# Rows sorted by expert for the second network; zeroing from 112 partitions, output scatters unordered, row numbers copied by VectorE

## The chip, the cores and the metric

The kernel runs on one core of a Trainium2 chip, in a single launch. The core has five engines, each with its own instruction stream: TensorE (PE: matmuls, and PEld for loading their weights), VectorE (DVE), ScalarE (ACT), GpSimd (POOL) and SyncE (SP, which here issues most DMAs). Engines wait for one another through semaphores; 16 DMA engines move data between DRAM and the on-chip memory (SBUF). Matmul results land in PSUM banks, from which VectorE or ScalarE take them. The metric is device time in microseconds (us) of one execution; lower is better.

## The reference, cut to what matters

```python
attn_out = _attn_ref(r, k, v, w, a, b)          # a recurrence over 768 steps, 4 x 8 heads of 40
x = attn_out.transpose(0, 2, 1, 3).reshape(3072, 320)

# first network: each token goes to one of 8 experts (320 -> 1024 -> 320)
logits = x @ w_gate
expert_idx = argmax(logits, 1)
probs = softmax(logits);  gate_w = probs[i, expert_idx[i]]
# token i is the pos[i]-th of its expert; dropped when pos[i] >= capacity (768)
h = maximum(disp[e] @ w1[e], 0);  y = h @ w2[e]
x[i] = gate_w[i] * y[expert_idx[i], pos[i]]     # 0 when dropped

# second network: one network for all tokens (320 -> 2048 -> 320)
h = x @ w_in
g = where(h > 0, h, exp(minimum(h, 0)) - 1)
out = g @ w_out                                 # float32, in the order of the tokens
```

## The kernel before

The program has three stretches. **Attention** (to about 445 us) works through 24 units of 128 tokens in an order written out by hand (`ORDER`, `slot(k)`): for each unit `x_out` gives 320 features and 8 router logits per token, `route` and `route_mm` find the token's expert and its row, and `scatter` writes the unit's 128 rows into the DRAM buffer `disp` with an indirect DMA on GpSimd (one row number per partition, from `SLOT`). `disp` has a region of rows for each expert. `zero_d` clears the first 448 rows (`SL`) of each region beforehand, and `zero` clears, in six pieces between units 8 and 13, the rows of the buffer `yd` that lie behind the first 8 x 448.

**The first network** (455 to 695 us) has one block of 448 rows per expert, in four groups of 112. Block.`load` fetches the rows from `disp`; `turn` and `prep` transpose them on TensorE (12 transposes, four after each of three steps, `pt`) and split them into a high and a low part, `XH`, `XL`, and `XS` for the last 64 features (float32 accuracy out of reduced-precision matmuls). A block has 8 steps f of 128 hidden units: `s1(f)` is 8 matmuls of 448 columns into a bank `ph`; `relu` makes the parts `H` (ScalarE) and `L` (VectorE); `s2`, two steps later, takes for each of the four row groups three matmuls of 320 columns (weights: 112 columns of `H` or `L`; moving: the second weight matrix) into the four banks `po`. After the last step the four banks are copied to `Y`, and one DMA writes them to `yd`, at 448 rows per expert. The weights come from DRAM in halves of an expert (`Weights.fetch`), and `split` makes their high part (ScalarE, L777) and low part (GpSimd, L780), a quarter per step, two halves ahead. In the same steps VectorE converts the second network's weights from 64-bit to 32-bit floats (`Convert.pieces`, L853 to L865), and `gates()` computes in small pieces each token's gate and the row of `yd` (`ROW`) that holds its result.

**The second network** (from 704 us) has six blocks of 512 tokens with 16 steps each, in the order of the tokens. `load` gathers the 4 x 128 rows by `ROW` out of `yd` (four indirect DMAs on GpSimd, L1158), VectorE multiplies them by the gate (L1163), and `turn` and `prep` transpose and split as before. `elu` is the activation; its last subtraction `L` is on GpSimd (L1008) except in the first five steps. `s2` runs three steps behind. The outputs leave from SP, two groups at a time (L1169). Both networks are driven by `run(blocks, ...)`, each by a call of its own: the second call begins with `bl[0].start()`, which loads, transposes and splits the first block with nothing beside it.

Engines work in program order. `experts` calls `extra(b, f)` at the end of each step, so the place of an instruction in its engine's queue is set by block and step. `overflow()` repeats the work for experts with more than 448 rows; with these data its loop does not run.

Of the kernel before, what the change touches and what calls it, by code (L numbers as in the profile page):

```python
# [20 lines left out]
D = 320  # L21
NTOK = 3072
SL = 448
ES = 8 * SL
NU = 24
# [92 lines left out]
def attention(tc, nc, e_in, v_tok, d_in, wg, disp, cst, ring, early, early_w, cv, cap):  # L118
# [12 lines left out]
    sh = [ring.tile(i, F32) for i in range(4)]  # L131
# [10 lines left out]
    zr = sh[0][:, 2578:2738]  # L142
# [412 lines left out]
    def x_out(u):  # L555
# [6 lines left out]
        XO = wk.tile([128, 4, 80], F32, tag="XO", name="XO", bufs=4)  # L562
        st["XO", u] = XO
        nc.scalar.copy(XO, pv[:, :, 0:80])
        yield
        nc.vector.tensor_reduce(cst["lg"][:, u], pv[:, :, 80:88].rearrange("p j e -> p e j"), axis=AX.X, op=ALU.add)
# [5 lines left out]
    def route(u, n=2):  # L572

        c, r = u // 2, slice(u % 2, u % 2 + n)
        LG, MX = cst["lg"][:, u:u + n], cst["mx"][:, u:u + n]
# [29 lines left out]
    def scatter(u):  # L605
        x = nc.gpsimd.indirect_dma_start(
            out=disp, out_offset=bass.IndirectOffsetOnAxis(ap=cst["slot"][:, u:u + 1], axis=0),
            in_=st.pop(("XO", u)).rearrange("p j e -> p (j e)"), in_offset=None).ins
# [5 lines left out]
    def zero(dst):  # L614
        nc.sync.dma_start(out=dst.rearrange("(p i) d -> p (i d)", p=128).rearrange("p (x d) -> p x d", d=160),
                          in_=zr.unsqueeze(1).to_broadcast([128, 8, 160]))

    def zero_d(e):
        nc.sync.dma_start(out=disp[e * ES:e * ES + SL, :].rearrange("(p i) d -> p (i d)", p=112).rearrange("p (x d) -> p x d", d=160),
                          in_=zr[0:112].unsqueeze(1).to_broadcast([112, 8, 160]))  # L620
# [6 lines left out]
    def warm(n):  # L627
        w = early_w.H[0]
# [37 lines left out]
    for k in range(KR, NU + 1):  # L666
# [17 lines left out]
def consts(p):  # L684
# [8 lines left out]
    c["lg"] = p.tile([128, 24, 8], F32, name="LG")  # L693
    c["mx"] = p.tile([128, 24], F32, name="MX")
    c["oh"] = p.tile([128, 2, 8, 12], BF, name="OH")
    c["slot"] = p.tile([128, 24], I32, name="SLOT")
    c["gate"] = p.tile([128, 24], F32, name="GATE")
    c["row"] = p.tile([128, 24], I32, name="ROW")
    c["pos"] = p.tile([128, 24], F32, name="POS")
    c["epos"] = p.tile([128, 24], F32, name="EPOS")  # L700
    c["tok"] = p.tile([128, 24], F32, name="TOK")
# [14 lines left out]
def set_rest(nc, c):  # L716
# [5 lines left out]
    for e in range(8):  # L722
        g.memset(c["desc"][:, e:e + 1], float(8 - e))
        g.memset(c["ebase"][:, e:e + 1], float(ES * e))
# [603 lines left out]
```

## Time and profile before

| | us |
|---|---|
| median of 3 runs (lowest to highest) | 1073.83 (1069.45 to 1074.62) |
| profiled execution, device time | 1081.15 |
| its span, first to last instruction | 1078.9 |
| TensorE busy in the span | 981.8 (91%) |
| VectorE, ScalarE, GpSimd busy | 711.3, 497.6, 635.5 |
| chain of waits: TensorE's share, at the lines of `s1` (L964) and `s2` (L979 to L981) | 44%; 21%, 8%, 7%, 7% |

The profile is one execution; its own time lies 7.3 us above the median. A matmul's shown duration includes its way through the array, so successive matmuls overlap: their pace is read from their start times, not from their durations. "Idle before, <- X" names what ended an engine's wait.

### The profile page before, as it was taken

Reading aid. Unit: us, or ns where it says so; the run is one execution under the profiler, and the core shown is the slowest. Engines: PE = TensorE matmul, PEld = TensorE weight load, DVE = VectorE, ACT = ScalarE, POOL = GpSimd, SP = SyncE. Lnnn points to the kernel's source line nnn. Section 1 sums busy time; section 2 is a strip of 40 time slices with the busy share of each in tenths; the row PEclk is TensorE's granted clock in tenths of the full one; section 3 lists DMA queues with packets and bytes.
Section 4 is the critical chain, followed back from the end, with each engine's and each line's share of the span. In section 5 each row is a group of like instructions: output and inputs, shape, how many; then the busy total and the mean of one; then the engine's idle time right before and its main releaser. Section 6 shows DMA issues by size and latency. Waiting matters only on the chain.

```text
span 1078.9 us, 25743 instructions
## 1 busy us (share of the span) xinstructions
PE 981.8 (91%) x10319; PEld 897.1 (83%) x10319; DVE 711.3 (66%) x1232; ACT 497.6 (46%) x968; POOL 635.5 (59%) x932
## 2 busy tenths in 40 slices
PE   5868888799799899888999999789999999999995
PEld 5758887798788789678999999768899899989985
DVE  8856657687664666538899972157675757666563
ACT  4646544566454334242343434345555554555452
POOL 4757839798986713474777776763444435353332
PEclk9858988899899989999999999979999999999998
DMA  6769675588674855575888774410100101010101
GB/s 165 157 171 206 156 145 92 145 143 201 148 176 94 200 137 114 160 188 150 239 237 227 197 203 144 140 43 7 38 13 7 44 1 49 1 50 1 26 1 28
DMA packets 187160, 125.21 MB, mean 116 GB/s; under 512 B 102776, under 2 KB 174968, under 8 KB 185400
## 3 DMA queue, kind: packets, MB, share of 16 engines
q1 hardware_dynamic: 182964, 106.53, 40.6%
q0 software_dynamic: 3168, 11.03, 3.2%
q10 hardware_dynamic: 900, 5.93, 2.2%
q8 instruction: 83, 1.36, 0.6%
q14 instruction: 45, 0.37, 0.1%
HBM read 86.73 MB, written 36.72 MB: 114 GB/s over the span
## 4 chain that ended last, share of the span: by engine, by line
PE 44%; DVE 4%; issue 3%; DMA 3%; POOL 2%; ACT 1%; SPq 1%; POOLq 0%; ACTq 0%; DVEq 0%
PE ph L964 21%; PE po L981 8%; PE po L980 7%; PE po L979 7%; POOL L L1008 1%; PE pt L937 1%; DMA ring<-in_w_dram 1%; DMA S<-in_w_in_dram 1%; DVE L L994 1%; SPq L796 1%; DVE E L854 1%; DVE N L853 1%; POOL ring L780 0%; DVE N L864 0%; DVE M L862 0%
## 5 line engine op out<-in xcount | busy, mean ns | idle before, releaser
L780 POOL TENSOR_TENSOR ring<-ring,ring 128x176 fp32r<-128x176 f32 x320 | 200.1, 660 | 76.5 <-ACT ring L777 76.5
L1008 POOL TENSOR_TENSOR L<-E,H 128x512 fp32r<-128x512 f32 x91 | 121.7, 1337 | 195.1 <-ACT H L1007 182.5
L981 PE MATMUL po<-ring,L 128*128 128x320 f32 (+1 forms) x640 | 199.0, 311 | 4.9 <-DVE L L994 3.8
L979 PE MATMUL po<-ring,H 128*128 128x320 f32 (+1 forms) x640 | 197.5, 309 | 2.6 <-ACT H L993 2.6
L980 PE MATMUL po<-ring,H 128*128 128x320 f32 (+1 forms) x640 | 198.0, 309 | 0.0
L964 PE MATMUL ph<-XH,ring 128*128 128x512 f32 (+1 forms) x640 | 173.7, 393 | 2.6 <-DVE L L994 1.8
L1001 ACT ACTIVATE E<-N 128x512 f32<-128x512 f32 x96 | 60.7, 633 | 143.5 <-DVE N L1000 76.2
L964 PEld LDWEIGHTS ph<-XH,ring 128*128 128x128 f32 x640 | 113.8, 191 | 15.6 <-DVE L L994 2.0
L350 POOL TENSOR_TENSOR X<-X,ring 128x60 f32<-128x60 f32 (+19 forms) x170 | 117.3, 690 | 13.3
L979 PEld LDWEIGHTS po<-ring,H 128*128 128x128 f32 (+1 forms) x640 | 117.0, 183 | 8.3 <-ACT H L993 2.9
L981 PEld LDWEIGHTS po<-ring,L 128*128 128x128 f32 (+1 forms) x640 | 117.0, 183 | 8.1 <-DVE L L994 6.6
L980 PEld LDWEIGHTS po<-ring,H 128*128 128x128 f32 (+1 forms) x640 | 117.0, 183 | 6.2
L1000 DVE TENSOR_SCALAR N<-ph 128x512 f32<-128x512 f32 x96 | 66.2, 689 | 74.6 <-PE ph L964 72.9
L964 PE MATMUL ph<-XS,ring 128*128 128x512 f32 (+1 forms) x320 | 97.7, 386 | 0.1
L964 PE MATMUL ph<-XL,ring 128*128 128x512 f32 (+1 forms) x320 | 97.1, 385 | 0.0
L348 POOL TENSOR_TENSOR ring<-X,ring 128x60 f32<-128x60 f32 (+19 forms) x108 | 68.6, 636 | 44.2 <-DMA ring<-dab 24.9
L1005 DVE SCALAR_TENSOR_TENSOR M<-E,M 128x512 f32<-128x512 f32 x96 | 84.9, 884 | 0.2 <-ACT M L1002 0.2
L274 PE MATMUL sc<-ring,ring 128*128 128x128 f32 x384 | 63.5, 322 | 20.7 <-ACT ring L261 15.0
L274 PEld LDWEIGHTS sc<-ring,ring 128*128 128x128 f32 x384 | 56.3, 227 | 22.5 <-ACT ring L261 15.2
L1006 DVE SCALAR_TENSOR_TENSOR E<-ph,M 128x512 f32<-128x512 f32 x96 | 66.4, 692 | 9.5
L964 PEld LDWEIGHTS ph<-XS,ring 128*128 128x128 f32 x320 | 60.5, 189 | 11.1 <-DVE XS L954 0.5
L964 PEld LDWEIGHTS ph<-XL,ring 128*128 128x128 f32 x320 | 60.6, 189 | 10.9
(224 smaller groups left out, 1841.0 us busy)
## 6 DMA issues: line engine op xcount, KB each, us to landing
ring<-in_w_dram SPq DMA_DIRECT2D x16, 640.0 KB
ring<-in_w_dram SPq DMA_DIRECT2D x32, 256.0 KB
RVU<-in_d_in_dram SPq DMA_DIRECT2D x48, 160.0 KB
dab<-AB SPq DMA_DIRECT2D x24, 256.0 KB
ring<-in_e_in_dram ACTq DMA_DIRECT2D x18, 321.6 KB
ring<-w SPq DMA_DIRECT2D x4, 1408.0 KB
disp<-ring SPq DMA_DIRECT2D x8, 560.0 KB
ring<-in_w_dram SPq DMA_DIRECT2D x32, 128.0 KB
```

The costliest lines, as they stand in the source:

```text
L274: nc.tensor.matmul(p[:, 128 * i:128 * i + 128], kb[:, q].rearrange("p x t -> p (x t)"), A[:, :, q, :], start=True, stop=True)
L348: nc.gpsimd.tensor_tensor(tv, X[:, 0:n, s:s + 1].to_broadcast([128, n, m]), N[:, s:s + 1, s + 1:e].to_broadcast([128, n, m]), op=ALU.mult)
L350: nc.gpsimd.tensor_tensor(X[:, 0:n, s + 1:e], X[:, 0:n, s + 1:e], tv, op=ALU.subtract)
L780: s.nc.gpsimd.tensor_tensor(s.L[g][:, q], R[:, q], s.H[g][:, q].bitcast(F32), op=ALU.subtract)
L964: nc.tensor.matmul(p, l, r[:, 0:s.T], start=i == 0, stop=i == len(seq) - 1)
L979: nc.tensor.matmul(o, H[:, c], hb, start=f == 0, stop=False)
L980: nc.tensor.matmul(o, H[:, c], lb, start=False, stop=False)
L981: nc.tensor.matmul(o, L[:, c], hb, start=False, stop=last)
L1000: nc.vector.tensor_scalar(N, p, 0.0, None, op0=ALU.min)
L1005: nc.vector.scalar_tensor_tensor(out=M, in0=E, scalar=1.0, in1=M, op0=ALU.add, op1=ALU.mult)
L1006: nc.vector.scalar_tensor_tensor(out=E, in0=p, scalar=0.0, in1=M, op0=ALU.max, op1=ALU.add)
L1008: eng.tensor_tensor(L, E, H.bitcast(F32), op=ALU.subtract)
```

## The change

The second network takes its rows sorted by expert instead of in token order, and its results are put in place when they are written.

- Each row scattered into `disp` becomes 329 wide (`RW`): 320 features, the token's number and its 8 logits. The number stands in column 0 of `lg`, and a VectorE copy per unit puts the nine values beside the features. A region's first 448 rows are left free now; `zero_d` and the scatters use the next ones.
- The first network's second product is made transposed (`Turned.s2`): features are the weights' columns and the block's 448 rows stream, 8 matmuls of 448 columns. The weight halves lie in one tile with high and low part side by side (`paired`), so that one matmul takes the high and the low part of the last 64 features.
- The gate is computed per block from the 8 logits (`soft`) and multiplied onto the expert's input by ScalarE; for the first expert it is multiplied onto the output (`late_gate`). `gates()` runs only in the overflow loop.
- The outputs go to the DRAM buffer `xt`, already transposed (row 320 holds the token numbers), at the columns where the expert begins in the sorted order. That start is loaded into registers of SP (`bi`, seven numbers). `zero_x` clears `xt` in three pieces (after units 8, 10 and 12) from 112 partitions, in place of six pieces of `yd`.
- The second network's six blocks (`sorted_block`) stand in the same list as the experts', in one `run`. They load columns of `xt`, need no gather, scale or transposes, and write with one indirect DMA per 128 rows on GpSimd, with the token numbers copied to integers by VectorE. The scatters are declared to be independent of each other; a small memset on GpSimd follows each.

```diff
-        XO = wk.tile([128, 4, 80], F32, tag="XO", name="XO", bufs=4)
+        XO = wk.tile([128, RW], F32, tag="XO", name="XO", bufs=4)
...
+        nc.vector.tensor_reduce(cst["lg"][:, u, 1:9], pv[:, :, 80:88].rearrange("p j e -> p e j"), axis=AX.X, op=ALU.add)
+        nc.vector.tensor_copy(XO[:, D:RW], cst["lg"][:, u])
...
+    def zero_x(j):
+        nc.sync.dma_start(out=xt[112 * j:112 * j + 112, :].rearrange("p (x d) -> p x d", d=220),
+                          in_=zr[0:112].unsqueeze(1).to_broadcast([112, 16, 220]))
...
-        if 8 <= k < 14:
-            i = k - 8
-            zero(cst["yd"][8 * SL + 512 * i:8 * SL + 512 * i + 512, :])
+        if 8 <= k < 14 and k % 2 == 0:
+            zero_x(k // 2 - 4)
...
+            nc.tensor.matmul(p0, hb[:, a], H, start=first, stop=False)
+            nc.tensor.matmul(p1, hb[:, b], H, start=first, stop=False)
+            nc.tensor.matmul(p0, lb[:, a], H, start=False, stop=False)
+            nc.tensor.matmul(p1, lb[:, b], H, start=False, stop=False)
+            if not last:
+                nc.tensor.matmul(p2, s.W.tail(f), H, start=first, stop=False)
+            nc.tensor.matmul(p0, hb[:, a], L, start=False, stop=last)
+            nc.tensor.matmul(p1, hb[:, b], L, start=False, stop=last)
+            nc.tensor.matmul(p2[0:64], hb[:, c], L, start=False, stop=False)
+            if last:
+                nc.tensor.matmul(p2, s.W.tail(f), H, start=False, stop=True)
...
+                    nc.scalar.copy(Y[:, 0], p0)
+                    nc.vector.tensor_copy(Y[:, 1], p1)
+                    nc.scalar.copy(half, p2[64:128])
+                    nc.vector.tensor_tensor(Y[0:64, 2], p2[0:64], half, op=ALU.add)
...
+    def soft(s, tag="s"):
...
+        nc.vector.tensor_reduce(g, lg, axis=AX.X, op=ALU.max)
+        nc.vector.tensor_tensor(x, lg, g.unsqueeze(2).to_broadcast([112, 4, 8]), op=ALU.subtract)
+        nc.scalar.activation(out=x, in_=x, func=AF.Exp)
+        yield
+        nc.vector.tensor_reduce(g, x, axis=AX.X, op=ALU.add)
+        nc.vector.tensor_scalar(g, g, 1e-9, None, op0=ALU.add)
+        nc.vector.reciprocal(g, g)
...
+            for i in range(4):
+                nc.scalar.mul(s.X[0:112, i, 0:D], s.X[0:112, i, 0:D], g[:, i:i + 1])
...
+                def store(Y, e=e):
+                    c = bass.ds(over["base"][e - 1], SL) if e else slice(0, SL)
+                    nc.sync.dma_start(out=xt[0:256, c].rearrange("(k p) n -> p k n", p=128), in_=Y[:, 0:2])
+                    nc.sync.dma_start(out=xt[256:D, c], in_=Y[0:64, 2])
+                    nc.sync.dma_start(out=xt[D:D + 1, c], in_=Y[64:65, 2])
...
+            bl += [sorted_block(g) for g in range(6)]
+        run(bl, extra)
...
+            nc.sync.dma_start(out=s.X[:, 0:2], in_=xt[0:256, c].rearrange("(k p) n -> p k n", p=128))
+            nc.sync.dma_start(out=s.X[0:64, 2], in_=xt[256:D, c])
+            f = ap.tile([128, 4], F32, tag="idf", name="idf")
+            with nc.allow_non_contiguous_dma("a token's number a row"):
+                nc.sync.dma_start(out=f, in_=xt[D:D + 1, c].rearrange("o (i p) -> p (o i)", p=128))
...
+            nc.vector.tensor_copy(s.id, f)
...
+            x = nc.gpsimd.indirect_dma_start(
+                out=out, out_offset=bass.IndirectOffsetOnAxis(ap=B.id[:, i:i + 1], axis=0),
+                in_=Y[:, i], in_offset=None, bounds_check=NTOK - 1, oob_is_err=False).ins
...
+            nc.gpsimd.memset(gap, 0.0)
...
-            nc.vector.tensor_reduce(ri, rg, axis=AX.X, op=ALU.add)
-        yield
-        over["n"] = nc.values_load(ri[0:1, 0:1], min_val=1, max_val=7)
...
+        _, over["base"] = nc.values_load_multi_w_load_instructions(bi[0:1, 0:7], (mybir.EngineType.SP,), min_val=0, max_val=NTOK)
+        yield
+        over["n"] = nc.values_load(ri[0:1, 0:1], min_val=1, max_val=8)
...
-    second()
```

Three places of the order follow. The first is TensorE at the seam between the networks, in the program before: `po` is the last product of the last expert, `pt` the transposes of the second network's first block, `ph` its first product.

```order
L981 MATMUL po<-ring_8724,L 112x320
L937 MATMUL pt<-ident,X 128x128 x2
L937 MATMUL pt<-ident,X 64x128
L937 MATMUL pt<-ident,X 128x128 x2
L937 MATMUL pt<-ident,X 64x128
L937 MATMUL pt<-ident,X 128x128 x2
L937 MATMUL pt<-ident,X 64x128
L937 MATMUL pt<-ident,X 128x128 x2
L937 MATMUL pt<-ident,X 64x128
L964 MATMUL ph<-XH,ring_8848 128x512 x2
```

In the changed program the same place reads, from the last expert's second-last product to its last:

```order
L1024 MATMUL po<-L,ring_8675 64x448
L969 MATMUL ph<-XH,ring_8803 128x512 x4
L969 MATMUL ph<-XL,ring_8803 128x512 x2
L969 MATMUL ph<-XS,ring_8803 128x512 x2
L1016 MATMUL po<-H,ring_8675 128x448
L1017 MATMUL po<-H,ring_8675 128x448
L1018 MATMUL po<-H,ring_8675 128x448
L1019 MATMUL po<-H,ring_8675 128x448
L1022 MATMUL po<-L,ring_8675 128x448
L1023 MATMUL po<-L,ring_8675 128x448
L1024 MATMUL po<-L,ring_8675 64x448
L1026 MATMUL po<-H,ring_8675 128x448
```

The twelve transposes are gone, and the second network's first products stand among the last expert's second products. The rows of `po` also show the new shape: eight matmuls of 448 columns a step where there were twelve of 320.

The second place is GpSimd at a block boundary of the second network after the change (`L<-E,H` is the subtraction of `elu`, 16 a block):

```order
L1097 TENSOR_TENSOR L<-E,H 128x512 x16
L1264 DMA out_dram<-Y,id 3072x320
L1270 MEMSET gap 128x1
L1264 DMA out_dram<-Y,id 3072x320
L1270 MEMSET gap 128x1
L1264 DMA out_dram<-Y,id 3072x320
L1270 MEMSET gap 128x1
L1264 DMA out_dram<-Y,id 3072x320
L1270 MEMSET gap 128x1
L1097 TENSOR_TENSOR L<-E,H 128x512 x16
```

Before, GpSimd had the four gathers of a block there, one between two subtractions; now it has four scatters in a row, each waiting for its quarter of `Y`, with the next block's subtractions behind them.

The third place is SP in the first network after the change, where the register load of the column starts stands between the weight conversion's DMAs (`S`, `w`) and a fetch of weights (`ring`):

```order
L826 DMA S_6886<-in_w_out_dram 128x640
L831 DMA w_75<-E 512x1x128
L1337 TENSOR_LOAD bi
L1337 ISA x14
L826 DMA S_7030<-in_w_out_dram 128x640
L831 DMA w_75<-E 512x1x128
L802 DMA ring_7069<-in_w_dram 128x4x128 x2
```

It is new; the load of the loop count `ri` that follows it on all engines was there before.

## Rows read from the trace of the kernel before

**Rows 1.** Busy us by engine (PE, PEld, DVE, ACT, POOL), clock, DMA share, GB/s.

```profile
0.00:440.00 440.00, 376.13 (x6870) 347.02 (x6870) 301.33 (x583) 212.38 (x468) 294.87 (x495) 0.89 0.68 153
509.00:617.00 108.00, 106.31 (x638) 100.27 (x637) 99.18 (x153) 42.85 (x77) 83.66 (x119) 1.00 0.80 218
644.00:671.00 27.00, 27.00 (x166) 25.91 (x165) 7.20 (x12) 11.62 (x21) 19.02 (x36) 1.00 0.52 167
692.00:712.00 20.00, 10.75 (x46) 7.89 (x45) 4.50 (x9) 2.39 (x5) 7.57 (x11) 0.70 0.24 70
760.00:1000.00 240.00, 240.00 (x1344) 216.06 (x1343) 159.54 (x232) 123.61 (x216) 102.74 (x81) 1.00 0.08 23
```

**Rows 2.** TensorE's timeline at the seam: start, us, operation, idle before.

```profile
695.37 0.31 PE L981 MATMUL po<-ring,L 128*112 128x320 f32 x1
...
703.57 0.90 PE L937 MATMUL pt<-ident,X 128*128 128x128 f32 x3 [7.89 <-DVE X L1163]
...
708.52 2.14 PE L964 MATMUL ph<-XH,ring 128*128 128x512 f32 x4 [0.25 <-ACT XH L953]
...
712.17 1.73 PE L964 MATMUL ph<-XH,ring 128*128 128x512 f32 x4
...
714.66 1.10 PE L964 MATMUL ph<-XH,ring 128*128 128x512 f32 x4
```

**Rows 3.** GpSimd's timeline at the seam: the first gather.

```profile
700.21 1.00 POOL L1158 DMA_INDIRECT X<-yd,ROW  x1 [5.43 <-DMA yd<-Y]
```

**Rows 4.** TensorE's timeline, one step of the first network.

```profile
612.03 0.97 PE L964 MATMUL ph<-XH,ring 128*128 128x448 f32 x4
...
613.65 0.30 PE L979 MATMUL po<-ring,H 128*112 128x320 f32 x1
...
615.41 0.97 PE L964 MATMUL ph<-XH,ring 128*128 128x448 f32 x4
```

**Rows 5.** The chain of waits in the second network: start, us, what.

```profile
742.85 1.87 PE ph L964 x8
...
755.07 1.86 PE ph L964 x8
...
758.69 1.87 PE ph L964 x8
```

**Rows 6.** TensorE's timeline in the second expert: its waits for VectorE.

```profile
486.36 0.40 PE L981 MATMUL po<-ring,L 128*112 128x320 f32 x1 [2.38 <-DVE L L994]
...
501.37 1.41 PE L964 MATMUL ph<-XH,ring 128*128 128x448 f32 x4 [1.84 <-DVE L L994]
```

**Rows 7.** VectorE's operations: one line's, and two groups (busy us, mean ns | idle).

```profile
L1191 DVE COPY cnt<-pc x1: 150/150/150, 502.0 to 502.0; 128x8 f32<-128x8 f32 x1
...
L988 DVE COPY Y<-po 112x320 f32<-112x320 f32 x16 | 7.7, 489 | 15.9 <-PE po L981 15.8
...
L954 DVE TENSOR_TENSOR XS<-pt,XS 64x448 fp32r<-64x448 f32 x8 | 4.9, 617 | 4.2 <-ACT XS L953 4.0
```

**Rows 8.** GpSimd: scatters in attention (ns min/median/max), two of them, the subtraction of `elu`.

```profile
L606 POOL DMA_INDIRECT disp<-XO,SLOT x24: 958/1014/1482, 138.8 to 446.7; - x24
...
DMA to landing us min/median/max: 2.8/5.0/6.0
...
320.20 1.02 POOL L606 DMA_INDIRECT disp<-XO,SLOT  x1 [0.30 <-ACT AB L278]
...
321.52 0.97 POOL L606 DMA_INDIRECT disp<-XO,SLOT  x1 [0.19 <-issue]
...
L1008 POOL TENSOR_TENSOR L<-E,H 128x512 fp32r<-128x512 f32 x91 | 121.7, 1337 | 195.1 <-ACT H L1007 182.5 <-PE ph L964 10.4 <-PE po L981 2.1
```

**Rows 9.** SP: the load of a register (ns min/median/max).

```profile
L1200 SPq TENSOR_LOAD <-ri x1: 485/485/485, 518.9 to 518.9; - x1
```

**Rows 10.** The end: timeline of TensorE and of SP.

```profile
1067.34 0.31 PE L981 MATMUL po<-ring,L 128*128 128x320 f32 x1
...
1067.26 2.60 SPq L1169 DMA_DIRECT2D out_dram<-Y  x4
```

More of the change, by code (lines that the diff above doesn't have):

```diff
@@ L967, in s1, with bank @@
             return p, H, L
+        def bank(s, n):
+            return [ps.tile([128, 512], F32, tag=f"po{i}", name="po", bufs=1) for i in range(n)]
         def s2(s, f, HL):
@@ new lines, in rows, with load @@
+    def rows(src, gate=True):
+        def load(s, now):
+            s.X = s.XF[:, 0:4 * RW].rearrange("p (i d) -> p i d", i=4)
+            for i in range(4) if now else (slice(0, 4),):
+                nc.sync.dma_start(out=s.X[0:112, i], in_=src[:, i])
+            yield
+            if not gate:
+                return
+            yield
+            g = yield from soft(s)
+            for i in range(4):
+                nc.scalar.mul(s.X[0:112, i, 0:D], s.X[0:112, i, 0:D], g[:, i:i + 1])
+            yield
+        return load
@@ L1073, in gates @@
-        nc.vector.tensor_tensor(cst["row"], y, epos, op=ALU.add)
-        nc.vector.tensor_tensor(cst["gate"].rearrange("p (c b) -> p b c", b=2), z.rearrange("p (c b) -> p b c", b=2), kp, op=ALU.mult)
-    def run(blocks, extra, back=1):
+        nc.vector.scalar_tensor_tensor(out=t, in0=t, scalar=over["cap"], in1=OH, op0=ALU.is_lt, op1=ALU.mult)
+        kp = T("kp", [128, 24])
+        nc.vector.tensor_reduce(kp.rearrange("p (c b) -> p b c", b=2), t.rearrange("p b e c -> p b c e"), axis=AX.X, op=ALU.add)
@@ L1078, in run @@
+        nc.vector.tensor_scalar(pos, pos, float(-SL), None, op0=ALU.add)
+        nc.vector.scalar_tensor_tensor(out=epos, in0=eb, scalar=1.0 / 8, in1=pos, op0=ALU.mult, op1=ALU.add)
+        return kp, pos, epos
+    def run(blocks, extra):
         n = len(blocks)
@@ L1139, in experts @@
         gen = [iter(())]
+        first = iter(()) if dyn else late_gate(bl[0])
+        next(first, None)
         def extra(b, f):
+            if b >= 8:
+                next(final, None)
+                return
+            if b == 0 and f > 1:
+                next(first, None)
             i, ph = divmod(8 * b + f, 4)
@@ L1169, in store @@
                         nc.sync.dma_start(out=out.rearrange("(B r) d -> r B d", B=2)[r:r + 64], in_=Y[64 * b:64 * b + 64, i - 1:i + 1])
-            bl.append(Block(W2, load, elu, store, scale))
+            bl.append(Block(W2, load, elu, store, back=3))
         bl[0].start()
-        if again:
-            for g in range(4):
-                W2.fetch(g)
-                for _ in W2.split(g) if g < 3 else ():
-                    pass
+        for g in range(4):
+            W2.fetch(g)
+            for _ in W2.split(g) if g < 3 else ():
+                pass
         last = W2.split(3)
@@ L1259, in more @@
                 next(rest, None)
-    gt, ct = gates(), counts()
-    next(gt)
+    one = over["one"] = ap.tile([128, 8], F32, name="one", bufs=1)
+    nc.gpsimd.memset(one, 1.0)
+    start = over["start"] = ap.tile([128, 6], F32, name="begin", bufs=1)
+    for i in range(4):
+        nc.gpsimd.iota(start[:, i:i + 1], pattern=[[0, 1]], base=112 * i, channel_multiplier=1, allow_small_or_imprecise_dtypes=True)
+    nc.gpsimd.memset(start[:, 4:5], 0.0)
+    nc.gpsimd.memset(start[:, 5:6], float(SL))
+    cst["turn"] = ap.tile([128, 1], F32, name="turn", bufs=1)
+    nc.gpsimd.memset(cst["turn"], 0.0)
+    ct = counts()
     experts(0, more=more)
```

347 lines of the change are left out of this document (196 added, 151 removed).

## The prediction, made before the changed kernel ran

> **What bounds the kernel now.** I read the busy time by stretch first. From 760 to 1000 us TensorE is busy all the time at the full clock (2.4 GHz), and in the first network it lacks 1.7 us of 108 and later none [rows 1]. So behind 455 us time is saved only by fewer or shorter matmuls, or where TensorE stands still. The largest hole is at the seam, where it is busy for 10.75 of 20 us, at a clock of 0.70 [rows 1]. TensorE's timeline shows that hole in pieces [rows 2]: the last product of the first network starts at 695.37, then 7.89 us of waiting, transposes, and first products that take 3.65 us (708.52 to 712.17) instead of 1.87 [rows 5]. GpSimd's timeline names the root: its first gather waited 5.43 us for the store of `yd` [rows 3]. Then I looked for a second limit. VectorE is busy 99.2 of 108 us while the weights are converted, and 7.2 of 27 when that is over [rows 1], so before 644 us a shorter TensorE step meets a VectorE that is nearly full. In attention VectorE has 301 of 440 us, and the DMA engines are 68% busy at 153 GB/s [rows 1].
>
> **The change part by part**, against the profiled 1081.15 us.
>
> *Seam.* Store, gathers, scale and transposes leave the path, since the second network's first block is loaded and split during the last expert. The last product ends at 695.37 + 0.15 = 695.52 by its pace (12 in 1.76 us [rows 4]); two first products of 1.87 [rows 5] would then end at 699.26. The third one starts at 714.66 [rows 2]. Gain 714.66 − 699.26 = 15.4, with the clock's share in it (TensorE had stood still for 7.89 us before the clock fell). Lower bound: as rival B. Nothing is late next by length: the first block's columns belong to the first experts, whose rows are in DRAM blocks earlier.
>
> *Transposes of blocks 2 to 6.* Three steps with them take 755.07 − 742.85 = 12.22 us, a step without 758.69 − 755.07 = 3.62 [rows 5]: 12.22 − 10.86 = 1.36 a block, times 5 = 6.8. TensorE is the bound there [rows 1], so all of it counts.
>
> *Second product transposed.* Now 12 products take 615.41 − 613.65 = 1.76 us; eight of 448 columns take 613.65 − 612.03 = 1.62 [rows 4]. The new product is eight of 448 columns: 1.62. Gain 0.14 × 64 steps = 9.0 at most. VectorE limits it. Per expert its two copies of 0.49 become a copy and an addition at 448 columns (0.62 each, as the 64 x 448 row): +0.26 [rows 7]; and five small gate operations of 0.15 (128 x 8) to 0.49 us (112 x 320) come in, at most 32 elements a row, so nearer the first: 5 × 0.17 = 0.85. Together 1.1 us. Eight steps shrink from 27.0 to 25.9 us, and VectorE needs 99.2 / 4 = 24.8 plus 1.1: 25.9. It sits on the edge, for some 45 of the 64 steps (from the second expert until before 644 us). I take a third of the gain as lost: +6, bounds 0 and 9. ScalarE gets four multiplications an expert and is busy for 42.9 of 108 us there [rows 1]: covered.
>
> By TensorE's paces in the Trainium skill ("TensorE: Matmul & The Clock Gate", Back-to-back issue gap: columns over 2.4 GHz plus about 2.5 ns) the two products would take an estimated 1.63 and 1.51 us, a gain of 7.5 instead of 9.0. The trace has 147 ns for 320 columns and 203 ns for 448 [rows 4], both above the page's 136 and 189, so the rows' 9.0 stands as the upper end.
>
> *`gates()` gone.* It ran on VectorE in the second expert, where TensorE waited 2.38 and 1.84 us for `L` [rows 6]. The first wait is behind the first conversion and stays; the second lies behind a backlog that `gates` helped to build. I take 1.5; bounds 0 and 4.2 (both).
>
> *XO copies.* 24 × 0.15 [rows 7] = 3.6 if all lay on the path; VectorE has idle time in attention [rows 1], so 0 is the other end. I take −1, as a part of the units wait for VectorE.
>
> *Wider rows and zeroing.* `zero_x` moves 3 × 1.58 MB where `zero` moved 6 × 0.655: +0.8 MB, about 5 us of transfer at 153 GB/s [rows 1], beside DMA engines that have a third of their time free, and from SP with half the issues. I take −0.5, bounds −4 and +1. Wider scatters add 9 in 320 columns and hide.
>
> *Register load on SP.* Seven values at 0.485 [rows 9] hold SP for 3.4 us, with the conversion's loads and weight fetches queued behind. Fetches run two halves ahead, so they cover most. I take −1, bounds −3.4 and 0.
>
> *Output scatters on GpSimd.* No scatter of outputs exists before; the nearest are the 24 of attention, of the same 128 rows: 1.01 us median, 1.48 longest, two in a row 1.32 apart with their memset [rows 8]. At a block boundary four of them stand ahead of a subtraction (1.34 [rows 8]) that the block's second `s2` needs. The first quarter of `Y` is ready 0.8 us before the old block's last product ends (three more row groups of 0.44, less a copy of 0.49), and `L` is needed 3.62 + 1.87 + 0.29 = 5.78 after it. TensorE waits 4p − 5.24 for a pitch p: 0.04 at 1.32, and 1.9 at the longest (1.48 + 0.30). Five boundaries: 0 to −9.4; I take −0.5, from the median row. In return the four gathers a block leave GpSimd.
>
> *Tail.* SP's last issues ended at 1067.26 + 2.60 = 1069.86 [rows 10]. Now the last scatter ends at 1067.65 − 0.8 + 4 × 1.32 = 1072.1; by landing (5.0 median, 2.8 least [rows 8]) it may add a little or nothing. I take −2.5, bounds −4.2 (at 1.78 each) and 0.
>
> Sum: 15.4 + 6.8 + 6 + 1.5 − 1 − 0.5 − 1 − 0.5 − 2.5 = 24.2. The profile would come to 1081.15 − 24.2 = 1057. It lies 7.3 above the median, and I put that down to nothing that the change touches: 1073.83 − 24.2 = 1049.6, **1050**.
>
> **The rivals.**
>
> A, *VectorE becomes the bound of the first network.* If it needs its 1.1 us on top of today's 27 per expert wherever the weights are converted (5.7 experts), the gain of those 45 steps goes (45 × 0.14 = 6.3, of which 3 are already taken off) and 5.7 × 1.1 = 6.3 come on top: 9.6 worse, 1059. For it: the sum of 25.9 leaves nothing over. Against it: part of VectorE's idle time is waiting for matmuls, which shrinks with the step.
>
> B, *the seam stays in another form.* `prep` now runs in an expert's last steps and ends one step (3.25 us) ahead of the next block, where it had three; loads of `xt` stand on SP behind weight fetches and stores with register addresses. If the first sorted block comes late, some 13 of the 15.4 are lost: 1063. Against it: the DMA engines are busy for only 0.24 of that stretch [rows 1].
>
> C, *more falls away than I count.* The whole 9.0, both waits of [rows 6], no loss from copies and register load: 3 + 2.7 + 1 + 1 = 7.7 better: 1042.
>
> D, *GpSimd's scatters hold up every boundary; slower than before.* Each boundary costs 4p − 5.24 and the tail 4 (p − 1.32): 24p − 31.5 in all. From p = 2.3 us this eats the whole gain. At twice the longest scatter and 0.30 (3.26) it is 46.7, and the time 1097. Against it: the scatters of attention keep to 0.96 to 1.48 us [rows 8], where VectorE is busy for 68% of the time [rows 1]; the second network's 159.54 of 240 [rows 1] is no more.
>
> The Trainium skill ("SBUF — State Buffer", SBUF: two separate sides) speaks for D and against this change: it says that a DMA issued from GpSimd needs descriptors written there, which VectorE locks out during certain of its operations, and that SP's DMAs escape this; a DMA of about 620 ns became about 3100. That would put p near 3.4, an estimate from the page, and the time near 1100. The trace of the scatters does not show it.
>
> **How the numbers follow.** Forecast 0.69, A 0.14, C 0.08, B 0.05, D 0.04. The bounds of the terms, added as squares, give the forecast its own range of 1044 to 1058. A and C belong in the range, B and D are left out, with the far end of A: 1038 to 1061. The kernel's runs tell about 0.5% from no change, that is 1068.5; forecast, A, B and C all lie under it, D above. Some of B with long scatters would end near no change. Faster 0.94, same 0.02, slower 0.04.
>
> **What would show it.** Seam: between the last `po` of an expert and the first `ph` of 512 columns TensorE's timeline has no hole, and the granted clock there is near 1.0; a wait for `X` or `XH` of some us would be B. Steps of the first network at 3.25 us, and at 3.4 with waits for `L` if A holds. No `pt` in the second network, and 3.62 a step throughout. GpSimd's scatters 1.3 apart with little waiting for `L` behind them; a pitch over 2 is D. From the last matmul to the span's end, 13 to 14 us instead of 11.3. My forecast falls if attention ends more than 4 us later than before, since I have priced its edits at 1.5.

## The result, and the profile after

The changed kernel took 1087.9 us (median of 4 runs) beside 1074.0 before on the same chip: 1.4% slower, ratio 1.0142 with an interval of 1.0101 to 1.0184. On a later occasion it was 1087.8 beside 1078.0, ratio 1.0079 (1.0044 to 1.0114). The forecast was 1050 us, 2% faster. The profiled execution has a span of 1090.2 us, 11.3 more than before. Cut at three places of TensorE's timeline, it reads (in us):

| | before | after | difference | forecast |
|---|---|---|---|---|
| start to the warm-up matmuls that follow attention | 443.2 | 451.4 | +8.3 | +1.5 |
| to the first product of the first network | 11.7 | 12.7 | +1.0 | 0 |
| to the third first product of the second network (with the seam) | 259.8 | 241.3 | −18.5 | −21.9 |
| to the end of the last product | 353.0 | 366.4 | +13.4 | −6.3 |
| to the end of the span | 11.3 | 18.4 | +7.1 | +2.5 |

So the seam gave what was forecast, the first network less, and the second network, attention and the tail (from the end of the last product to the end of the span) took more than that back. Busy time by engine, in the columns of [rows 1]:

```profile
509.00:617.00 108.00, 102.96 (x504) 88.69 (x503) 92.13 (x167) 51.59 (x97) 73.29 (x114) 0.98 0.78 221
692.00:712.00 20.00, 18.94 (x89) 15.99 (x87) 4.92 (x8) 8.33 (x14) 14.93 (x29) 1.00 0.32 105
760.00:1000.00 240.00, 230.61 (x1256) 204.96 (x1255) 149.32 (x209) 116.39 (x208) 106.91 (x95) 1.00 0.07 20
```

At the seam TensorE is now busy and its clock is full. But in the second network, where it was busy for 240.00 of 240 us [rows 1], it now lacks 9.4. TensorE's timeline at the seam (after, to be read beside [rows 2]):

```profile
699.85 0.36 PE L1024 MATMUL po<-L,ring 128*64 128x448 f32 x1
700.06 1.09 PE L969 MATMUL ph<-XH,ring 128*128 128x512 f32 x4
...
701.92 1.09 PE L969 MATMUL ph<-XH,ring 128*128 128x512 f32 x4
...
703.77 0.36 PE L1016 MATMUL po<-H,ring 128*128 128x448 f32 x1
...
705.41 1.09 PE L969 MATMUL ph<-XH,ring 128*128 128x512 f32 x4
```

No hole is left between the last expert's products (448 columns) and the next network's (512). Where TensorE waits instead stands in the list of waits (after, us in total, times, longest), `L1097` in the second network, `L1083` in the first, `L1029` at the seam:

```profile
PE po L989 <- POOL L L1097: 12.9, 15, 1.1
...
PE po L1022 <- DVE L L1083: 8.5, 6, 3.8
...
PE po L987 <- ACT Y L1029: 1.7, 1, 1.7
```

The start-to-start times of the second network's steps place the first of these. A plain step takes 3.62 us. In each of blocks 1 to 5 one or two steps near the end are long (4.72, or 3.95 and 4.99): 6.7 us over 3.62 in all. At four of the five block boundaries two steps are long (4.65 to 4.69, then 4.77 to 4.89), at the last one a single step (4.90): 10.2 us. The first block has 5.94, 3.89 and 3.77: 2.7 us. These sum to 19.6, and forecast and trace differ by 19.7 there.

In the first network an undisturbed step is 3.25 us instead of 3.37. But at the first of the three steps with transposes TensorE waits for the rows that ScalarE multiplies by the gate (ScalarE and TensorE in the fourth expert, after):

```profile
575.33 1.92 ACT L1076 ACTIVATE X<-X,g 112x320 f32<-112x320 f32 x4 [1.45 <-DVE g L1061]
```

```profile
576.22 1.41 PE L934 MATMUL pt<-ident,X 112*128 112x112 f32 x4
577.39 1.06 PE L969 MATMUL ph<-XH,ring 128*128 128x448 f32 x4
```

From the first of these four transposes to the next product 1.17 us pass. Before, it was 0.32 for most experts, and after the change it still is for the last one. For the six experts ahead of that one it is 0.57 to 1.18, in all 4.4 us over 0.32.

**The steps that split the next block.** All engines, first block (after):

```profile
747.74 0.62 ACT L1046 CAST XH<-X 128x512 fp32r<-128x512 f32 x1
...
747.91 1.30 POOL L1097 TENSOR_TENSOR L<-E,H 128x512 fp32r<-128x512 f32 x1 [3.33 <-PE po L988]
748.39 1.37 DVE L1047 TENSOR_TENSOR XL<-X,XH 128x512 fp32r<-128x512 f32 x1 [1.26 <-ACT XH L1046]
...
749.68 0.68 DVE L1089 TENSOR_SCALAR N<-ph 128x512 f32<-128x512 f32 x1
...
750.45 0.63 ACT L1090 ACTIVATE E<-N 128x512 f32<-128x512 f32 x1 [2.09 <-DVE N L1089]
...
751.84 0.62 ACT L1096 CAST H<-E 128x512 fp32r<-128x512 f32 x1 [0.24 <-DVE E L1095]
752.37 0.61 ACT L1046 CAST XS<-X 64x512 fp32r<-64x512 f32 x1
...
752.54 1.30 POOL L1097 TENSOR_TENSOR L<-E,H 128x512 fp32r<-128x512 f32 x1 [3.33 <-ACT H L1096]
753.01 1.37 DVE L1047 TENSOR_TENSOR XS<-X,XS 64x512 fp32r<-64x512 f32 x1 [1.26 <-ACT XS L1046]
```

This is a ring: VectorE's `XL` waits for ScalarE's `XH`, which stands behind `H`, and ends only after GpSimd's `L`, which needs `H` too; VectorE's next `N` stands behind `XL`; and the next `H` needs that `N`. One turn takes 752.54 − 747.91 = 4.63 us. `XL` takes 1.37 us. It starts while GpSimd's `L` runs and ends 0.54 to 0.55 after it (749.21 and 749.76; 753.84 and 754.38). Before, the same subtraction read PSUM and took 0.69 in those steps (a group of the kernel before: busy us, mean ns | idle):

```profile
L954 DVE TENSOR_TENSOR XL<-pt,XH 128x512 fp32r<-128x512 f32 x10 | 6.9, 691 | 13.3 <-ACT XH L953 13.3
```

It ran beside an `L` there too, and ended 0.16 us before it (before, GpSimd and VectorE):

```profile
749.32 1.29 POOL L1008 TENSOR_TENSOR L<-E,H 128x512 fp32r<-128x512 f32 x1 [1.77 <-ACT H L1007]
...
749.75 0.69 DVE L954 TENSOR_TENSOR XL<-pt,XH 128x512 fp32r<-128x512 f32 x1 [2.57 <-ACT XH L953]
```

**The boundary.** GpSimd, VectorE and TensorE at the first one (after):

```profile
770.35 1.29 POOL L1097 TENSOR_TENSOR L<-E,H 128x512 fp32r<-128x512 f32 x1 [1.77 <-ACT H L1096]
771.80 1.02 POOL L1264 DMA_INDIRECT out_dram<-Y,id  x1 [0.16 <-DVE Y L996]
...
775.70 0.97 POOL L1264 DMA_INDIRECT out_dram<-Y,id  x1 [0.19 <-issue]
...
776.73 1.28 POOL L1097 TENSOR_TENSOR L<-E,H 128x512 fp32r<-128x512 f32 x1
```

```profile
778.30 0.17 DVE L1261 CAST id<-idf 128x4 int32<-128x4 f32 x1 [4.73 <-DMA out_dram<-Y,id]
778.38 0.68 DVE L1089 TENSOR_SCALAR N<-ph 128x512 f32<-128x512 f32 x1
```

```profile
778.07 0.41 PE L989 MATMUL po<-ring,L 128*128 128x320 f32 x1 [0.80 <-POOL L L1097]
...
782.83 0.41 PE L989 MATMUL po<-ring,L 128*128 128x320 f32 x1 [0.88 <-POOL L L1097]
```

The scatters are 1.30 us apart, as forecast. But the first starts at 771.80, behind an `L` that ends at 771.64, though the copy that makes its quarter of `Y` had ended at 770.69. And VectorE stands still for 4.73 us before it copies the row numbers, until the scatters have landed.

### The profile page after: what moved, and what is told of

The parts are those of the page before. It is cut to its first block, busy times and chain, and to the rows that moved or that the text cites. A ratio compares the mean times of both kernels' runs of the same rounds, so it can differ in the third digit from the quotient of the medians.

```text
span 1090.2 us, 25387 instructions
## 1 busy us (share of the span) xinstructions
PE 975.8 (90%) x9995; PEld 872.1 (80%) x9995; DVE 713.0 (65%) x1262; ACT 514.6 (47%) x1011; POOL 645.8 (59%) x951
## 4 chain that ended last, share of the span: by engine, by line
PE 25%; POOL 11%; issue 9%; DMA 5%; DVE 4%; ACT 2%; SPq 1%; POOLq 0%; DVEq 0%; ACTq 0%
PE ph L969 12%; POOL L L1097 4%; POOL ring L781 4%; PE po L989 4%; DMA ring<-in_w_dram 3%; PE po L987 3%; PE po L988 3%; POOL out_dram L1264 2%; DMA w<-E 1%; SPq L802 1%; ACT ring L776 1%; DVE L L1083 1%; DMA S<-in_w_in_dram 1%; DVE E L860 1%; PE po L1022 0%
## 5 line engine op out<-in xcount | busy, mean ns | idle before, releaser
L781 POOL TENSOR_TENSOR ring<-ring,ring 128x64 fp32r<-128x64 f32 (+2 forms) x320 | 196.2, 649 | 85.4 <-ACT ring L776 85.4
L1097 POOL TENSOR_TENSOR L<-E,H 128x512 fp32r<-128x512 f32 x91 | 128.2, 1409 | 192.3 <-ACT H L1096 177.0
L969 PE MATMUL ph<-XH,ring 128*128 128x512 f32 (+1 forms) x640 | 171.1, 389 | 0.5 <-ACT XH L953 0.5
L989 PE MATMUL po<-ring,L 128*128 128x320 f32 x384 | 120.7, 314 | 13.0 <-POOL L L1097 12.9
L987 PE MATMUL po<-ring,H 128*128 128x320 f32 x384 | 119.0, 310 | 1.8 <-ACT Y L1029 1.7
L988 PE MATMUL po<-ring,H 128*128 128x320 f32 x384 | 118.7, 309 | 0.0
L989 PEld LDWEIGHTS po<-ring,L 128*128 128x128 f32 x384 | 72.2, 188 | 17.9 <-POOL L L1097 17.5
L1094 DVE SCALAR_TENSOR_TENSOR M<-E,M 128x512 f32<-128x512 f32 x96 | 78.2, 814 | 10.8 <-ACT M L1091 10.8
L987 PEld LDWEIGHTS po<-ring,H 128*128 128x128 f32 x384 | 72.1, 188 | 7.1 <-ACT Y L1029 2.2
L988 PEld LDWEIGHTS po<-ring,H 128*128 128x128 f32 x384 | 72.2, 188 | 4.1
L776 ACT CAST ring<-ring 128x704 fp32r<-128x704 f32 x80 | 61.3, 777 | 13.1 <-DMA w<-GE 5.5
L1096 ACT CAST H<-E 128x512 fp32r<-128x512 f32 x96 | 58.9, 613 | 11.0 <-DVE E L1095 10.6
```

Of the source, the lines that this page charges most:

```text
L776: s.nc.scalar.copy(B[:, 0:704], r)
L781: s.nc.gpsimd.tensor_tensor(B[:, to], r[:, q], B[:, q].bitcast(F32), op=ALU.subtract)
L969: nc.tensor.matmul(p, l, r[:, 0:s.T], start=i == 0, stop=i == len(seq) - 1)
L987: nc.tensor.matmul(o, H[:, c], hb, start=f == 0, stop=False)
L988: nc.tensor.matmul(o, H[:, c], lb, start=False, stop=False)
L989: nc.tensor.matmul(o, L[:, c], hb, start=False, stop=last)
```

## Experiments

Single executions of one code scatter: attention ended at 440.6 to 451.4 us in nine profiles with the clearing as changed, and at 443.2 and 439.0 in two of before. The stretch from the second network's third step to the last product does not: 364.6 to 367.6 us in five profiles that have the changed code there (in one of them the last block stores from SP). So the second network and the tail are judged by the traces, attention by medians beside the kernel before on the same chip.

**The changed kernel again**, as a reference.

> The changed kernel as it is, beside the others on the same chip, because the first network and attention together differ by up to 10 us between profiled executions of the same code (attention ended at 438 to 451 us in five of them). Expected by all theories: 1083 to 1092 us, last matmul to end of span 18 to 19 us, boundaries with 4.7 and 4.8 us steps.

Measured: 1087.8, that stretch 364.6, tail 18.4.

**Three buffers for the row numbers.**

```diff
-            s.id = ap.tile([128, 4], I32, tag="id", name="id")
+            s.id = ap.tile([128, 4], I32, tag="id", name="id", bufs=3)
```

> The changed kernel with three buffers instead of two for the integer row numbers. Theory 2: VectorE's copy of the next block's row numbers waits until the scatters that read the old ones in the same buffer have landed (4.73 us of VectorE idle at the first boundary), and that makes the second of the two long steps at each of four boundaries (4.77 instead of 3.62 us): that step falls to 3.6 to 3.9, total gain 3.5 to 4.6, 1083 to 1085 us. Rival: only the four scatters in GpSimd's queue ahead of the subtraction L matter; the two long steps stay at 4.7 and the time at 1088.

VectorE no longer waits, and a boundary has one long step (4.97) instead of two. The boundary steps take 3.6 us less than in the first profile of the changed kernel and 2.9 less than in the second. With two buffers the copy for the block after next goes into the buffer that the scatters are still reading, and waits for them. The whole stretch takes 363.1. (1083.1 us, ratio to before 0.9998, 0.9957 to 1.0039.) The other long step remains, so the scatters' place in the queue is a second cause.

**The subtraction one step later.**

```diff
             for k, (h, l) in enumerate(s.parts()):
                 x = s.X[0:(128, 128, 64)[k], k]
+                if late:
+                    nc.vector.tensor_tensor(late[0], late[1], late[2].bitcast(F32), op=ALU.subtract)
                 nc.scalar.copy(h, x)
-                nc.vector.tensor_tensor(l, x, h.bitcast(F32), op=ALU.subtract)
+                late = l, x, h
                 yield
```

> The changed kernel with the subtraction that makes XL and XS of the second network's blocks moved one step behind the copy that makes XH and XS. Theory 3: with both operands in SBUF that subtraction waits for GpSimd's subtraction L, which starts just ahead of it in the same step (1.36 us instead of 0.69), and with the wait for ScalarE it closes a loop of 4.6 us a step; one step later it starts ahead of L: 0.7 us each, steps of 3.62 in place of the 1.1 to 1.7 us extra a block, gain 5.5 to 8, 1080 to 1082.5 us. Rival: 1.36 us is what it takes from SBUF, whatever runs beside it: it stays at 1.36, and the gain is 0 to 4.

All steps that split a block are 3.62 to 3.63, and the stretch takes 357.1, 9.3 less than in the first profile of the changed kernel and 7.5 less than in the second (1081.0 us, ratio 0.9961, 0.9918 to 1.0004). The expectation was 5.5 to 8; the first long step of a boundary fell too, from 4.69 to 4.21. The subtraction (here `XL`, ns least, median, most; the changed kernel, then this one):

```profile
L1047 DVE TENSOR_TENSOR XL<-X,XH x12: 837/1362/1368, 686.8 to 994.3; 128x512 fp32r<-128x512 f32 x12
```

```profile
L1048 DVE TENSOR_TENSOR XL<-X,XH x12: 681/683/996, 687.0 to 986.4; 128x512 fp32r<-128x512 f32 x12
```

Same operands, both in SBUF: 0.68 us when it does not meet `L`, so the 1.36 was waiting, not the operation. The rival falls.

**Output stores from SP**, and the same for the last block alone.

```diff
-            x = nc.gpsimd.indirect_dma_start(
-                out=out, out_offset=bass.IndirectOffsetOnAxis(ap=B.id[:, i:i + 1], axis=0),
...
+            r = 512 * g + 128 * i
+            nc.sync.dma_start(out=out[r:r + 128], in_=Y[:, i])
```

> The changed kernel with its output stores as plain DMAs from SP, 128 rows each, in the order in which the rows are sorted (the rows are not put in the order of the tokens). Theory 4: scatters cost 2.2 us at four of the five boundaries (two steps of 4.7), and at the end 18.4 us from the last matmul to the end of the span instead of 11.3: boundaries fall to 3.62 a step and the tail to 11 to 13, gain 14 to 16, 1072 to 1074 us. Rival: the tail's length comes from something else at the end of the program and stays: gain 8 to 10.

> The changed kernel with the last block's outputs written by plain DMAs from SP in the sorted order (its 512 rows are not put in the order of the tokens); the other five blocks scatter. If the long tail comes from the four scatters at the very end (their issue, 5 us, and their landing), it falls from 18.4 to 9 to 11 us. If any scatter of outputs in the program makes the end long, it stays above 15.

Without scatters all boundary steps are 3.62, the stretch 353.3 and the tail 9.5 (1067.8 us, ratio 0.9842). That is more than expected, and part of it comes from elsewhere: the steps that split a block became shorter too (in each of blocks 2 to 5 one of 4.00, where there had been one of 4.72, or 3.95 and 4.99). So the two losses are not independent, and the 6.7 and 10.2 us above divide them by place, not by cause. With scatters in all blocks but the last the tail is 10.0. So the last block's scatters make the tail long, and scatters elsewhere do not.

**Scatters spread over four steps**, with both edits above: one scatter at the end of each of steps 2 to 5, behind that step's `L`.

```diff
+                if todo:
+                    q, Y, i = todo.pop(0)
+                    q(Y, i)
```

> The changed kernel with three buffers for the row numbers, the subtraction for XL and XS one step later, and the scatters of a block's four row groups put one at the end of each of the next block's steps 2 to 5, behind the subtraction L (the last block's four stay together). Theory of the boundary (four scatters in a row behind one L stand ahead of the L that TensorE needs first; the row numbers' buffer comes next): all steps of blocks 2 to 6 take 3.62 to 3.65 us, the second network from its third step to the last matmul 349 to 351 us instead of 366.4, 15 to 17 us less than the changed kernel. Rival, a scatter itself slows GpSimd's or VectorE's work beside it: steps with a scatter stay 0.3 us or more longer, gain under 12.

> The kernel with the scatters spread over four steps once more (three buffers for the row numbers, subtraction for XL and XS one step later), as the reference for the three others on the same chip. Expected: 15 us below the changed kernel's place, that is 4 to 7 us below the kernel before.

> The kernel best1 again, as the reference on the same chip: 0.985 to 0.996 of the kernel before.

GpSimd after the first boundary (first of these runs):

```profile
760.33 1.69 POOL L1102 TENSOR_TENSOR L<-E,H 128x512 fp32r<-128x512 f32 x1 [2.64 <-ACT H L1101]
762.18 1.02 POOL L1272 DMA_INDIRECT out_dram<-Y,id  x1 [0.16 <-issue]
...
763.79 1.70 POOL L1102 TENSOR_TENSOR L<-E,H 128x512 fp32r<-128x512 f32 x1 [0.48 <-ACT H L1101]
765.65 1.01 POOL L1272 DMA_INDIRECT out_dram<-Y,id  x1 [0.16 <-issue]
```

From the second block on all steps are 3.62 to 3.63, those with a scatter too, so the rival falls. GpSimd's `L` takes longer in the first of these runs (1.85 us in the median instead of 1.30), but no step does. The stretch takes 352.1 and 349.4 us, 14 to 17 less than with the scatters in a row. 1072.5 us stands beside 1087.8 for the changed kernel on the same chip. Beside before: 0.995 (0.9913 to 0.9986), 0.9863 (0.9824 to 0.9901) and 0.986 (0.981 to 0.991) on three occasions. So this version is faster than both kernels, than before by 0.5 to 1.4%.

**Without the overflow loop**, from the spread version.

```diff
-    overflow()
```

> The kernel best1 without the overflow loop, which these data never enter. In all runs 12 to 14 us pass between GpSimd's last instruction and the end of the span, whether it ends before TensorE or 4.7 us after it. If that is GpSimd's way past the loop's code, the tail (last matmul to end of span) falls from 18.5 to 9 to 13 us and the time by 6 to 9. If it is the scatters' landing and a fixed end, the tail stays at 16 to 18.5.

The last instructions of TensorE and GpSimd in the changed kernel, in this one, and GpSimd's in the kernel before:

```profile
1071.47 0.31 PE L989 MATMUL po<-ring,L 128*128 128x320 f32 x1
...
1076.11 0.11 POOL L1270 MEMSET gap<- 128x1 f32 x1
```

```profile
1046.20 0.31 PE L989 MATMUL po<-ring,L 128*128 128x320 f32 x1
...
1050.83 0.11 POOL L1278 MEMSET gap<- 128x1 f32 x1
```

```profile
1065.44 0.39 POOL L1214 IOTA rb<- 128x1 f32 x4
```

With the loop, GpSimd's last instruction stands 14.0 us before the end of the span (1090.2 − 1076.2) in the changed kernel and 13.1 in the kernel before; without it 5.4 (1056.3 − 1050.9). In all profiles with the loop this distance is 11.7 to 14.3 us, whether GpSimd ends 2.2 us ahead of TensorE or 4.4 behind it. Without the loop the tail falls to 9.8, and the kernel takes 1058.2 us beside 1065.6 with it on the same chip (ratios to before 0.9827 and 0.986, intervals overlapping, so the gain is read from the tail). So what follows GpSimd's last instruction is mostly due to the loop's code. It lay beside TensorE's last products; with four scatters behind them it begins 4.4 us after TensorE's end. What that time consists of was not measured.

**Attention: the clearing.** Left out of the changed kernel (z0) and of the spread version (bz0); in six halves of the pieces (z6); later (bzlate); from 128 partitions (bz128); and doubled in the kernel before (b2x). The clearing calls:

```diff
-        if 8 <= k < 14 and k % 2 == 0:
-            zero_x(k // 2 - 4)
```

> The changed kernel without zero_x (xt is not cleared; every column that is read is written by the experts). Theory 1: the three zeroing DMAs of 1.54 MB, twice to three times the size of the old pieces, hold up the small round trips of attention, and that is most of the 8.3 us by which attention ended later (warm-up matmuls at 454.0 us instead of 445.7): here they start at 440 to 447 us and the kernel takes 1076 to 1081 us. Rival: the 24 copies on VectorE or the rows of 1316 bytes cost those 8 us: the warm-up starts at 451 to 454 and the kernel takes 1085 to 1088.

> The changed kernel with the zeroing of xt in six pieces of 0.79 MB (after units 8 to 13) instead of three of 1.58 MB. Theory 1a, the size of one piece holds up attention's round trips: most of what leaving the zeroing out gained comes back, 6 to 11 us less than the changed kernel on the same chip. Theory 1b, what costs is the volume of small descriptors (880 bytes) between attention's own transfers: 0 to 3 us less.

> The same kernel as best1b without the clearing of xt (which these data do not need). If the clearing is what makes attention longer, it is 8 to 13 us faster than best1b and attention ends at 433 to 441 us; if it is not, 0 to 3 us.

> The same kernel as best1b with the clearing in six pieces of 0.79 MB after units 13, 14 and 15 (two each), where the DMA engines were busy for 0.38 of the time (335 to 365 us) instead of 0.6 to 1.0 at units 8 to 13. If the clearing costs because it meets full DMA engines, nearly all of the gain without clearing comes: 6 to 12 us faster than best1b. If it costs by its volume wherever it stands, or by holding up round trips at any place: 0 to 4.

> The kernel best1 with xt cleared in six pieces of 0.79 MB from 128 partitions in descriptors of 616 bytes (after units 8 to 13), the form that the kernel before used for its buffer. If the 112 partitions (or the piece size of 1.58 MB) make the new clearing dear, it is 3 to 7 us faster than best1; if volume decides, within 2 us of it.

> The kernel before with twice its clearing: after each of the six pieces of 0.655 MB a second one of the same form into a buffer that nothing reads. If a megabyte cleared in attention costs what leaving out 4.73 MB gained in the changed kernel (about 7.5 us, 1.6 a MB), it is 5 to 8 us slower than before, and the new clearing is then only 1 to 2 us dearer than the old one. If pieces of this form hide and only the new form costs, it is within 2 us of before.

Beside the spread version on the same chip, leaving the clearing out gave 7.5 us (1068.8 to 1061.3, ratios to before 0.9863 and 0.9806, intervals that overlap a little), with attention's end at 436.2; z0 had 1076.9 and 438.3. The late form gave nothing (1069.8, ratio 0.9863), 128 partitions nothing (0.992 beside 0.986), six halves 3.3 us beside the changed kernel (1.0061 beside 1.0079, intervals overlapping). Doubling the old one cost 0.87% (0.59 to 1.16), 9.4 us for 3.93 MB, above the 5 to 8 expected: 2.4 us a MB, where leaving out 4.73 MB gave 1.6 a MB. So a MB cleared in attention costs time, and no form or place that was tried was clearly cheaper. But the new clearing is larger by only 0.8 MB, 1.3 to 1.9 us at these prices.

**Attention: the copies and the wider rows.** The copies on GpSimd instead of VectorE (bxo); and, in the kernel before, rows 328 wide with 24 copies and the wider clearing of `disp` (bwide):

```diff
-        nc.vector.tensor_copy(XO[:, D:RW], cst["lg"][:, u])
...
+        nc.gpsimd.tensor_copy(st["XO", u][:, D:RW], cst["lg"][:, u])
```

```diff
-        XO = wk.tile([128, 4, 80], F32, tag="XO", name="XO", bufs=4)
+        XO = wk.tile([128, 328], F32, tag="XO", name="XO", bufs=4)
...
+        nc.vector.tensor_copy(XO[:, D:328], cst["lg"][:, u])
```

> The same kernel as best1b with the copy of a unit's nine values beside its features made by GpSimd just ahead of its scatter instead of by VectorE. If the 24 copies on VectorE (0.15 us each) lie on attention's path: 1 to 4 us faster; if they hide: within 1.5 us.

> The kernel before with attention's other edits alone: the rows scattered into disp are 328 wide (320 features, 8 logits; 1312 bytes instead of 1280), with the 24 copies on VectorE and the wider clearing of disp; the experts load the 320 features of them, and everything behind is as before. If wider rows and copies make attention longer, it is 4 to 9 us slower than before; if they hide, it is within 2 us.

> The kernel before once more, for a second profile of its attention (the first ended it, by the start of the warm-up matmuls, at 443.2 us, in an execution 7 us above the median). Attention of the changed kernel ended at 440.6 to 451.4 us in its profiles. If it is really some 8 us longer there, this profile has it at 434 to 441; if single executions only scatter, 441 to 450.

Moving the copies shows nothing (ratio 0.9874 beside 0.9863). Wider rows with copies cost 0.22% (−0.04 to 0.47), some 2.4 us, not clear of zero. The second profile of before ended attention at 439.0. Nine profiles of the new attention average 446.0, two of the old one 441.1: a difference of some 5 us, of which the clearing's 1.9 at most and the rows' 2.4 would be the larger part. With this scatter the rest can't be told from chance, and attention's share stays the least settled.

## Why the prediction was wrong, point by point

Four steps of its working failed: that all of the transposes' time counts, that the scatters start when `Y` is ready and keep no one waiting through their buffer, that the program ends as long after the last scatter as it had ended after SP's last issue, and that ScalarE's multiplications are covered. Attention was priced too low, for reasons that stay partly open. Its range was too narrow by its own bounds as well: 1058 comes out only without the scatters' −9.4, and with it 1062; the measured 1087.9 lies far outside either.

- **Seam, 15.4 forecast: right.** It closed as described, at full clock. (The clock before had fallen within the wait of 7.89 us and not after it: granted 1.00 from 695.6 to 699.8, 0.50 from 700 to 713.) The first block then lost 2.7 us (step 5.94): the last expert's results leave their PSUM bank late, because ScalarE's copy of them (712.08) stands behind two weight splits and a step's activation, and the first split began after 4.73 us of idle time (709.16), and `po` needs the bank (1.7 us in the list of waits). No run took this wait away.
- **Second product transposed, `gates()` and the register load, 6.5 together: some 1.5 measured.** With the seam, the stretch gave 18.5 instead of 21.9, and the cut flatters it: the last expert's last second product (707.27 to 708.91, 1.6 us) now lies behind it. From its first product to the end of its last the first network took 695.5 − 454.8 = 240.7 us; now it takes 708.9 − 464.1 = 244.8, of which three first products of the second network are 5.6: 239.2. The undisturbed step came as forecast (0.12 × 64 = 7.9 us). What failed is "covered", said of ScalarE's four multiplications an expert. It was argued from ScalarE's busy time, but the multiplications stand between the gate and the transposes, and TensorE waited for them (4.4 us, above). Waits for VectorE's `L` grew as well, from 5.6 us to 8.5. VectorE was busy for 92 of 108 us instead of 99, so rival A's full engine did not come. The register load held SP for some 3.7 us (510.3 to 514.0), and no wait of TensorE for a DMA is seen behind it. All this is read from the traces; no run took these waits away.
- **Transposes, 6.8 forecast, 0.1 measured: the step that failed** is "TensorE is the bound there, so all of it counts", argued from TensorE's busy share over 240 us. TensorE did set the steps of 3.98 to 4.09 (its products follow one another there without a gap), but the ring stood close behind: with the 0.69 us that the subtraction took from PSUM, the turn of 4.63 would be 3.95, an estimate, and already longer than 3.62. With the source in SBUF instead of PSUM the subtraction waited for GpSimd's `L`, and the ring grew to 4.63 a turn. The cost was 6.7 us beside 5 × 1.36 = 6.8 before. The prediction asked what the removed work cost, and not what the replacing subtraction would meet. One step's distance removed the cost (the run with the subtraction one step later).
- **Scatters, −0.5 forecast, −10.2 measured.** The pitch (1.30 beside 1.32) was right; two steps of the working were not. "The first quarter of `Y` is ready 0.8 us before" was taken for the scatter's start, but GpSimd was still in the preceding `L`: 771.80 instead of some 770.5, so that 4p − 5.24 becomes 4p − 3.9, a wait of 1.3 at p = 1.30 instead of 0 (0.80 measured, in a step that is 1.07 longer). And the row numbers' copy, which depends on the buffer that the scatters read, was not priced at all: 0.7 to 0.9 a boundary (2.9 to 3.6 over four, by the run with three buffers). The run with the scatters spread removed both. This is rival D's mechanism at a pitch of 1.3, not at 2.3: D had been priced by the scatters' own length alone.
- **Tail, −2.5 forecast, −7.1 measured.** The scatters' end was right (1076.2, 4.4 after the last product). Wrong was the part after it: 14.0 us instead of the 9.0 that followed SP's last issue, since the time that follows GpSimd's last instruction starts only then.
- **Attention, −1.5 forecast, −8.3 in this profile, about −5 on average.** The clearing was priced at 0.5 for 0.8 MB; doubling the old one showed 2.4 a MB. A third of the DMA engines' time being free does not hide it. By its own sign, attention's end more than 4 us later, the forecast fell. The rest is open.
- **Warm-up stretch, 0 forecast, −1.0**: not looked into.

The sum of the shortfalls in the profile: 6.7 + 9.7 + 2.7 + 0.6 (left over in that stretch, to which the cut adds 1.6) + 4.6 + 3.4 + 6.8 + 1.0 = 35.5, which is 24.2 + 11.3.

The Trainium skill ("SBUF — State Buffer", SBUF: two separate sides) was drawn on for a rival and bore on another place. Its warning that descriptors for GpSimd's DMAs starve did not show: the 24 output scatters took 0.97 to 1.21 us. VectorE was idle for more than half of their time, so this is no hard test. The same section says that a VectorE operation with two operands in SBUF and a GpSimd operation that reads SBUF take turns for the whole instruction. This case's trace agrees: each time they met, `XL` or `XS` ended 0.54 to 0.55 us after `L` (two rows above), though not to the tenth, since alone they take 0.68.

## What to carry to other kernels

When an edit takes work off the bounding engine, write down what the step's other engines form without it: a ring of engines that wait for one another in program order can hold the step as long as the removed work did, and one step's distance between producer and consumer opens it. Work put on an in-order queue is priced from what already stands in the queue and from the buffers it keeps busy, not by its own length; spreading it, one piece a step, made it free here. A busy share does not show what stands on the path: ScalarE had time to spare in the first network, and its multiplications ahead of the transposes held TensorE up all the same. And here the end of the program was set by GpSimd, whose last instruction had the longest way to the end.

## What the runs showed of the hardware that was not expected

- A subtraction with both operands in SBUF took 0.68 us alone and 1.36 beside GpSimd's subtraction, ending 0.55 us after it; from PSUM, beside the same subtraction, it had taken 0.69.
- GpSimd's last instruction was followed by 11.7 to 14.3 us to the end of the span with an untaken loop behind it, and by 5.4 without.
- Writing zeros to DRAM during attention cost 1.6 to 2.4 us a MB (left out and added), with the DMA engines 68% busy [rows 1].
